# A linear attention and a squared-ReLU MLP on one core: where query loads, key-value products and output stores stand in the program

## The chip, the core and the metric

The kernel runs on one core of a Trainium2 chip. The core has a matrix engine (TensorE, PE in the profile), three engines for elementwise work (VectorE or DVE, ScalarE or ACT, GpSimd or POOL), a SyncE (SP) that in this kernel does nothing but issue transfers, and 16 DMA engines that carry them out. The metric is the device time of one execution in microseconds (us); lower is better. All data are fp32 (the two weight matrices arrive as float64 and are converted in the kernel).

## The reference

Two stages, one after the other, over 8 batches of 576 tokens, 8 heads of 64:

```python
kv  = np.einsum('bhsd,bhse->bhde', k, v)            # per batch and head: 64 x 64
out = np.einsum('bhsd,bhde->bhse', q, kv)
rms = np.sqrt(np.mean(out * out, axis=-1, keepdims=True) + 1e-06)
x   = out / rms * g_norm                            # then (B,H,S,D) -> (B*S, H*D): 4608 x 512
h   = x @ w_in                                      # 512 -> 2048
y   = np.maximum(h, 0.0) ** 2 @ w_out               # 2048 -> 512
```

## The kernel before, in words

**Strips.** The 4608 tokens are 36 tiles of 128, and 4 tiles make a strip; there are nine strips, s = 0 to 8. Each strip runs an up part (x times w_in) and a down part (the squared activations times w_out). Both are Strassen-like products: seven block products in place of eight. Strip 0 uses one level (plain in the up part), strip 1 one level up and two levels down, strips 2 to 8 two levels in both parts. The up part of a strip from 2 on has 55 slots (`up_slot`): slot 7n + 2i holds the i-th small product (8 matmul records in the trace) of set n, so each slot issues one or two of them, and PE needs 0.89 us for one. The down part has 14 steps (`down_deep`), two for each of seven products p in the order 4, 1, 2, 6, 5, 7, 3. Product p = 4 is begun inside the up part (slots 49, 51 and 53), and the last products of p = 3 run in slots 1, 3 and 5 of the next strip.

**Streamed weights.** Sums of weight blocks are computed once, written to DRAM and streamed back for each strip (`stream`, L787): seven transfers of 768 KB for the up part (L793), and for each p one of 768 KB (L799, `w_blk<-w_out`) and one of 1024 KB (L805, `w_blk<-w_deep`). There are four places for them, so a transfer waits on SP until PE has read the tile that was in its place. In the up part `stream()` is called in slots 5, 10, 17, 24 (the rest of the up weights), 31 (w_out of p = 4), 38 (w_deep of p = 4), 45 and 52.

**Attention beside it.** The attention of later tiles is a list of `slices`, written out by hand at L623 to L652, and `attend` (L655) hands them out between the steps: in strips 2 to 8 between slots 1 and 37, up to a goal (L1183) that also limits how many are handed out by each strip. In short:

- `T (b, p)` = `transposed_query`: query of batch b, head pair p, is transposed, for b >= 2 by DVE (L360); with p = 3 of an odd batch also the remaining 64 tokens of two batches (L364, `qT_rest`).
- `K (b, p...)` = `key_value`: k times v for one or two head pairs (L394), eight matmul instructions for 512 tokens and two for the last 64 tokens of the batch (`k_rest`, `v_rest`). After its last product it issues the loads of the next k and v, and with p = 3 `load_rest` for the next batch.
- `query`: q times kv for two tiles (`products_x`, L426), optionally with a K behind it; `mean_roots`, `normalized`: the rms and the scaling on DVE.
- `squares_x`, `send_x` (L570), `fetch_x` (L576): x is transposed through DRAM: DVE transposes 32 x 32 blocks, one transfer writes the tile, four read it back.

The last two slices of a batch's queries and the first of the next one stand so:

```python
        for pair in query_pairs(b):
            ahead = b + 1 < B and pair == query_pairs(b)[-1]
            slices.append((query, (pair, *((b + 1, 0, 1) if ahead else ()))))
...
            if ahead:
                fetch(1)
                slices.append((K, (b + 1, 2, 3)))
```

**Loads.** The pool `qkv` has two places each for q, k and v (L81). For b >= 2 a query tile is four transfers of 64 KB (L121: 32 partitions, rows of 128 bytes). They are not issued where they are asked for, but put on a list (`drip_queries`, L189) by T, two halves per tile, and handed out one half per step by `drip` (L183); the remaining tokens' queries (L167, `q_rest`) go on a second list. In the up part a half of a query load goes out at every slot as long as there is one, in the down part at every second step:

```python
                if i < n_up or i % 2:
                    drip(s == DEEP or i % 2 == 1)
```

`k_rest` holds two batches, one in each half of the partitions. The products over it run over all 128 partitions; `v_rest` has a copy for each parity whose other half is zero (memsets at L320 and L321), so that the other batch's half adds nothing.

**Outputs.** `out_rows` (L661) says which rows of the result the two tiles of an output block go to. For batches from 2 on the tokens of a tile are permuted in blocks of 32, and a block of two tiles is sent as four transfers (one per 32 partitions, 64 KB each), for each of four column and token halves of a strip.

**One queue.** All of these, weights, q, k, v, x and outputs, are issued by SP in program order. An issue that has to wait for a place holds up everything behind it.

## Time and profile before

| what | us |
|---|---|
| five runs | 937.71, 931.76, 932.73, 936.63, 933.51 |
| median | 933.51 |
| the profiled execution, whole | 937.71 |
| its span, first to last instruction | 935.9 |
| outside the span | 1.8 |
| PE busy in the span | 891.3 |
| DVE, ACT, POOL busy | 731.9, 318.5, 305.4 |

The profiled execution is the slowest of the five. The profile names groups of instructions by line, engine, operation and tiles (out<-in); it also lists who waited for whom, a timeline for each engine, and for stretches of time the busy time of each engine with the clock that PE was granted (1.00 is full speed) and the mean share of the 16 DMA engines in use. An entry "SPq" is the issue of a transfer, not the transfer: the time beside it is SP's, and the median time from issue to landing is a table of its own. An SP entry with x8 covers eight issues one after the other. Matmul records overlap by their pipelining, so the distance from one group's start to the next group's start tells more than the duration shown. Over half of the chain of work that ended last is PE in the lines of the up part and the down part (L1109 and L921).

### The profile page before, as it was taken

To read this page: it belongs to the slowest core of one execution; us is meant where nothing else is said; L and a number is where in the kernel's file an instruction comes from. 1 tells how busy PE (TensorE), PEld (TensorE's weight loads), DVE (VectorE), ACT (ScalarE), POOL (GpSimd) and SP (SyncE) were. 2 spreads that over 40 slices of the span, in tenths; PEclk is the share of its full clock that TensorE was granted. 3 is DMA by queue.
4 is the path that set the end of the run, shared out by engine and by line. 5 is a ranking of instruction groups with operands and counts; after the bars stand their busy time and mean duration, and the time that the engine had idled before them with its cause. 6 is when DMAs were issued, how large, how long until landed. Compare 5 with 4: busy or idle time off the path is not lost.

```text
span 935.9 us, 20822 instructions
## 1 busy us (share of the span) xinstructions
PE 891.3 (95%) x8246; PEld 831.8 (89%) x8246; DVE 731.9 (78%) x1258; ACT 318.5 (34%) x638; POOL 305.4 (33%) x315
## 2 busy tenths in 40 slices
PE   6999799899999999989999999869999999999998
PEld 5534688789989999989999999869999999999998
DVE  3899779678867996769678967649689957985886
ACT  3797432221025502360137012710155015302710
POOL 0000000920248404630456045510463147234700
PEclk8999899999999999999999999979999999999999
DMA  8689998979898696878877886868655875685375
GB/s 267 212 290 262 289 334 271 265 246 366 302 229 256 243 317 205 217 228 318 277 188 249 330 269 178 212 235 319 232 181 200 329 228 181 257 300 170 140 291 194
DMA packets 173810, 235.74 MB, mean 252 GB/s; under 512 B 85008, under 2 KB 138768, under 8 KB 165264
## 3 DMA queue, kind: packets, MB, share of 16 engines
q1 hardware_dynamic: 173392, 234.27, 77.2%
q8 instruction: 65, 1.06, 0.5%
q14 instruction: 33, 0.27, 0.1%
q10 hardware_dynamic: 320, 0.13, 0.1%
HBM read 197.66 MB, written 36.70 MB: 250 GB/s over the span
## 4 chain that ended last, share of the span: by engine, by line
PE 70%; DVE 14%; DMA 7%; issue 3%; SPq 3%; ACT 1%; POOL 1%; DVEq 0%; ACTq 0%; POOLq 0%
PE ps_B L921 21%; PE ps_A L921 16%; PE ps_A L1109 15%; PE ps_B L1109 7%; PE ps_C L1109 4%; DMA w_blk<-w_deep 2%; PE ps_A L700 2%; PE x_ps L426 2%; DVE gt L1121 2%; PE kv_ps L394 1%; DVE w_c L250 1%; SPq L121 1%; DVE snap L1121 1%; DMA w_out<-w_in 1%; DVE w_t L270 1%
## 5 line engine op out<-in xcount | busy, mean ns | idle before, releaser
L921 PE MATMUL ps_B<-w_blk,g_s 128*128 128x128 f32 x1024 | 127.5, 277 | 0.0
L921 PEld LDWEIGHTS ps_B<-w_blk,g_s 128*128 128x128 f32 x1024 | 121.8, 194 | 0.0
L921 PE MATMUL ps_B<-w_blk,gt 128*128 128x128 f32 x768 | 99.1, 278 | 11.4 <-DMA w_blk<-w_deep 10.8
L1109 PE MATMUL ps_A<-x_l,w_in 128*128 128x128 f32 x784 | 107.1, 281 | 0.3 <-ACT snap L1126 0.3
L921 PEld LDWEIGHTS ps_B<-w_blk,gt 128*128 128x128 f32 x768 | 92.6, 194 | 12.3 <-issue 11.1
L270 POOL TENSOR_TENSOR x_l<-xT 128x256 f32<-128x256 f32 x21 | 15.4, 736 | 262.1 <-PE ps_A L921 203.4
L1109 PEld LDWEIGHTS ps_A<-x_l,w_in 128*128 128x128 f32 x784 | 97.9, 196 | 1.0 <-ACT snap L1126 0.5
L921 PE MATMUL ps_A<-w_blk,g_s 128*128 128x128 f32 x768 | 93.6, 275 | 0.0
L921 PEld LDWEIGHTS ps_A<-w_blk,g_s 128*128 128x128 f32 x768 | 89.6, 192 | 0.0
L1121 POOL TENSOR_TENSOR snap<-snap,gt 128x512 f32<-128x512 f32 x35 | 45.8, 1310 | 126.6 <-ACT snap L1126 93.5
L1059 ACT ACTIVATE gt<-gt 128x512 f32<-128x512 f32 x112 | 69.6, 622 | 28.2 <-DVE gt L1121 28.2
L1126 ACT COPY snap<-ps_A 128x512 f32<-128x512 f32 x63 | 36.6, 582 | 122.6 <-PE ps_A L1109 109.4
L921 PE MATMUL ps_A<-w_blk,gt 128*128 128x128 f32 x576 | 72.2, 275 | 0.0
L1060 ACT ACTIVATE gt<-gt 128x512 f32<-128x512 f32 x112 | 70.6, 631 | 3.6
L936 DVE TENSOR_TENSOR o_sb<-o_sb,ps_B 128x256 f32<-128x256 f32 (+1 forms) x128 | 49.4, 386 | 26.7 <-ACT o_sb L937 19.4
L921 PEld LDWEIGHTS ps_A<-w_blk,gt 128*128 128x128 f32 x576 | 68.2, 192 | 0.0
L1121 DVE TENSOR_TENSOR gt<-ps_A,gt 128x512 f32<-128x512 f32 x49 | 32.8, 681 | 43.0 <-PE ps_A L1109 41.3
L1019 POOL TENSOR_TENSOR w_i<-w_in 128x512 f32<-128x512 f32 x7 | 9.3, 1332 | 161.6 <-DVE w_in L270 160.6
L1121 POOL TENSOR_TENSOR gt<-gt,snap 128x512 f32<-128x512 f32 x42 | 52.3, 1273 | 23.5 <-DVE snap L1121 23.5
L270 DVE TENSOR_TENSOR gt<-gt 128x2048 f32<-128x2048 f32 (+1 forms) x29 | 59.7, 2063 | 0.0
L937 ACT COPY o_sb<-ps_A 128x128 f32<-128x128 f32 x24 | 6.4, 265 | 145.7 <-PE ps_A L921 145.7
L1109 PE MATMUL ps_A<-x_l,w_blk 128*128 128x128 f32 x392 | 53.3, 280 | 1.8 <-POOL x_l L270 0.9
(176 smaller groups left out, 1842.6 us busy)
## 6 DMA issues: line engine op xcount, KB each, us to landing
w_blk<-w_deep SPq DMA_DIRECT2D x56, 1024.0 KB, 6.0
w_blk<-w_out SPq DMA_DIRECT2D x56, 768.0 KB, 5.6
w_blk<-w_in_deep SPq DMA_DIRECT2D x49, 768.0 KB, 5.2
raw<-in_moe_w_in_dram SPq DMA_DIRECT2D x16, 512.0 KB, 6.5
raw<-in_moe_w_out_dram SPq DMA_DIRECT2D x16, 512.0 KB, 6.3
k<-in_k_dram SPq DMA_DIRECT2D x29, 256.0 KB, 4.6
v<-in_v_dram SPq DMA_DIRECT2D x29, 256.0 KB, 4.9
x_d<-x_q SPq DMA_DIRECT2D x27, 256.0 KB, 3.7
```

The costliest lines, as they stand in the source:

```text
L121: eng.dma_start(out=t[ts(a, SQ)], in_=src[b, 2 * p + h, 0 : C * P, f : f + SQ].rearrange("(i k) f -> i k f", k=4 * C),)
L250: yield nc.vector.scalar_tensor_tensor(out=ci, in0=high, scalar=-(2**30), in1=ci, op0=ALU.bitwise_and, op1=ALU.bitwise_or)
L270: eng.tensor_tensor(out=out, in0=a, in1=b, op=ALU.subtract)
L426: nc.tensor.matmul(ps[half, r, i, ts(p, D)], lhsT=q[row, half], rhs=kvd[b, p][row, row], start=True, stop=True)
L700: nc.tensor.matmul(bank[BANK[p]][:, i, :], lhsT=lhsT(k), rhs=rhs(k), start=p in (1, 5, 2) and i == 0 and k == 0, stop=k == n - 1, skip_gro ...
L921: nc.tensor.matmul(chain[c][x][:, i, :], lhsT=a[:, f, :], rhs=w[:, f, :], start=x not in opened[c] and f == 0, stop=f == FQ // 2 - 1, skip ...
L936: add = lambda out, a, b: nc.vector.tensor_tensor(out=out, in0=a, in1=b, op=ALU.add)
L1059: nc.scalar.activation(o, o, AF.Relu)
L1060: nc.scalar.activation(o, o, AF.Square)
L1109: nc.tensor.matmul(ps[:, i, :], lhsT=w, rhs=rhs, start=j in (1, 2, 5) and i == 0, stop=True, skip_group_check=True)
L1121: add = lambda eng, out, a, b: eng.tensor_tensor(out=out, in0=a, in1=b, op=ALU.add)
L1126: nc.scalar.copy(t, ps)
```

## The change

Six edits, which together move instructions and change few: the number of matmuls is the same.

```diff
-                t = qkv_pool.tile([P, 4 * C, SQ], FP32, name=n, tag=n) if 0 in parts else main[n, b, p]
+                t = qkv_pool.tile([P, 4 * C, SQ], FP32, name=n, tag=n, bufs=3) if 0 in parts else main[n, b, p]
...
-    v_rest = const.tile([P, 2, H, D], FP32, name="v_rest")
+    v_rest = const.tile([P, H, D], FP32, name="v_rest")
...
-    nc.vector.memset(k_rest, 0.0)
-    nc.vector.memset(v_rest, 0.0)
...
+        if (b, p) == (1, NP - 1):
+            drip_queries()
...
-                    a, w = (tk[:, h, c, :], tv[:, h, c, :]) if c < C else (k_rest[:, 2 * p + h], v_rest[:, b % 2, 2 * p + h])
+                    a, w = (t[:, h, c, :] if c < C else r[half, 2 * p + h] for t, r in ((tk, k_rest), (tv, v_rest)))
...
-    slices += [(features, (last[0],)), (T, (2, 2)), (K, (2, 2, 3)), (T, (2, 3))]
+    slices += [(features, (last[0],)), (T, (2, 2)), (T, (2, 3)), (K, (2, 2, 3))]
     for b in range(2, B):
+        pairs = query_pairs(b)
+        for i, pair in enumerate(pairs):
+            left = len(pairs) - i
+            more = b + 1 < B
+            keys = (b + 1, *{2: (0, 1), 1: (2, 3)}[left]) if more and left < 3 else ()
+            fetch(1)
+            if i == 0 and b > 2:
+                slices += [(T, (b, p)) for p in (2, 3)]
+            slices.append((query, (pair, *keys)))
+            if more and left == 1:
+                slices.append((T, (b + 1, 1)))
             slices.append((mean_roots, (pair,)))
             fetch(1)
             slices.append((normalized, (pair,)))
+            if more and left == 2:
+                slices.append((T, (b + 1, 0)))
...
-                to += [(ts(k, SQ), both, rows[k, :, cs]) for k in range(4)]
+                to += [(slice(0, P), slice(t + j, t + j + 1), rows[:, :, c]) for j, c in enumerate(range(cs.start, cs.stop))]
...
-            goal = max(goal, min(ready[DEEP_UP] + 24 * (s - 1), *ahead[:1], len(slices)))
+            goal = max(goal, min(ready[DEEP_UP] + 22 * (s - 1), *ahead[:1], len(slices)))
...
-                if i < n_up or i % 2:
-                    drip(s == DEEP or i % 2 == 1)
+                if i % (2 if s == DEEP else 4) == 1 and i < min(n_up, 37) or i >= n_up and i % 3:
+                    drip(True)
```

In words: q has three places; the products over the last 64 tokens read only their own half of the partitions, with one `v_rest` and no memsets; K of the next batch goes with the last two queries of the batch in front, pairs 0 and 1 with the last but one and pairs 2 and 3 with the last, in place of pairs 0 and 1 with the last and pairs 2 and 3 behind it; a half of a query load goes out at every fourth slot up to slot 37 (every second step in strip 1) and at two of three steps of the down part; the goal of slices grows by 22 per strip in place of 24; and a block of two output tiles goes out as two transfers of 128 KB, one per tile, over all partitions, whose target is a pattern of 4 x 32 rows of 256 columns.

## The prediction

> **What bounds the kernel now.** The page first: PE is busy nearly the whole span, so time can only come out of the 44.6 us (935.9 - 891.3) in which it waits, and out of stretches in which it runs slowly.

> ```profile
> PE 891.3 (95%) x8246; PEld 831.8 (89%) x8246; DVE 731.9 (78%) x1258; ACT 318.5 (34%) x638; POOL 305.4 (33%) x315
> ```

> Then the list of waits of PE alone: whom it waited for, total, times, longest. Four of its larger entries are transfers or DVE work that the change moves.

> ```profile
> PE ps_B L921 <- DMA w_blk<-w_deep: 10.8, 2, 7.6
> PE kv_ps L394 <- DMA v_rest<-in_v_dram: 3.5, 2, 2.7
> PE kv_ps L394 <- DMA v<-in_v_dram: 3.3, 3, 1.3
> PE x_ps L426 <- DVE qT_rest L364: 1.9, 1, 1.9
> ```

> Third, the timeline of PE around the longest one, in strip 5. Look at the distance of starts: eight matmuls of this kind need 0.89 us elsewhere.

> ```profile
> 584.18 0.69 PE L394 MATMUL kv_ps<-v,k 128*64 128x64 f32 x16
> 587.53 0.34 PE L394 MATMUL kv_ps<-v_rest,k_rest 128*64 128x64 f32 x4 [2.66 <-DMA v_rest<-in_v_dram]
> ...
> 588.38 1.92 PE L1109 MATMUL ps_A<-x_l,w_blk 128*128 128x128 f32 x8
> 590.09 1.91 PE L1109 MATMUL ps_A<-x_l,w_in 128*128 128x128 f32 x8
> ...
> 607.98 1.06 PE L1109 MATMUL ps_B<-x_t,w_blk 128*128 128x128 f32 x8
> 616.64 2.05 PE L921 MATMUL ps_B<-w_blk,gt 128*128 128x128 f32 x8 [7.61 <-DMA w_blk<-w_deep]
> 618.48 1.92 PE L1109 MATMUL ps_A<-x_l,w_in 128*128 128x128 f32 x8
> 620.18 4.95 PE L921 MATMUL ps_B<-w_blk,g_s 128*128 128x128 f32 x32
> ```

> A wait costs more than itself. After the 2.66 us wait the next groups of eight start 1.71, 1.71 and 0.99 us apart: 1.7 us lost (0.82 + 0.82 + 0.10). After the 7.61 us wait it is 1.84, 1.70 and 4.79 (to 624.97) for 8, 8 and 32: 3.0 us lost; the windows give PE a clock of 0.81 in 600 to 620 us and 1.00 before the waits. After the third long one, 3.21 us at 410.8 in strip 3, it is 1.39, 1.71 and 3.96: 1.7 us lost. After the 1.86 us wait at 267 nothing is lost. [...]

> Fourth, why w_deep came late: SP's timeline.

> ```profile
> 581.62 0.63 SPq L153 DMA_DIRECT2D v_rest<-in_v_dram  x1
> ...
> 583.01 9.14 SPq L121 DMA_DIRECT2D q<-in_q_dram  x8
> ...
> 601.66 7.85 SPq L121 DMA_DIRECT2D q<-in_q_dram  x8
> 609.55 2.04 SPq L576 DMA_DIRECT2D xT<-x_d  x4
> 611.69 0.38 SPq L805 DMA_DIRECT2D w_blk<-w_deep  x1
> ```

> This w_deep is asked for in slot 38, whose matmuls start at 595.47; it is issued 15 us after the end of that slot, behind two bunches of eight query loads (9.1 and 7.9 us of SP). Strip 3 has the same picture: eight q between 395.25 and 402.72, xT x8 at 402.76, w_deep at 408.87. The bound that can be moved is thus SP's queue; PE's work cannot be.

> **The change, part by part.** The sum is for the profiled execution (937.7).

> *Strip 5, w_deep of p = 4: -10.6* (7.6 + 3.0). In the changed order only two query issues, two x_d and four xT stand between w_out (slot 31) and w_deep (slot 38): 2 x 0.62 + 2 x 0.38 + 4 x 0.45 = 3.8 us, plus up to 3.7 us (median landing of x_d) that xT waits. Slot 38 is 6.2 us (seven slots of 0.89) after slot 31 and 13.4 before slot 53, which needs the tile; with its median landing of 6.0 us it may be issued 7 us late. No more than four query loads stand in a row anywhere after strip 1.

> *Strip 3, the same: -4.9* (3.2 + 1.7). More stands there: xT x4, K's four loads, two rest loads, q x2, xT x4 = 1.8 + 1.7 + 1.3 + 1.2 + 1.8 = 7.8 us, again from slot 31: at most some 2 to 5 us late of 7. If that cover goes, the old stall returns here first.

> *Strip 5, K of batch 7: -4.4* (2.7 + 1.7). Its loads were issued from 578.3 on, nine us after their places came free, behind xT and q. In the changed kernel K (6, 2, 3) is in slot 9 and K (7, 0, 1) in slot 25, 14 us apart, with x_d and xT right ahead of the six loads; issue 3.0 and landing 5.8 fit.

> *Strip 2, qT_rest: -1.9.* T (3, 3) moves from slot 6 to slot 3, so on DVE it stands ahead of the output sums of slot 5, which hold it at 267.96 now; DVE idles from 258.5 to 263.1. The query itself moves to slot 5, PE at 264. Strip 1's first w_out: -0.5, by less in front of it.

> *Strip 1, K of batch 3: a new wait, +2.3.* Now K (2, 2, 3) waits twice, 1.29 and 0.93 us at 173.7 and 175.8, since its loads stand behind eight query issues; behind four, and one step later (1.73 us), it does not: -2.2. But K (3, 0, 1) now follows K (2, 2, 3) after one step and 64 small products (1.73 + 1.16 us), and takes its places. The rows of now for these very loads:

> ```profile
> 176.22 0.59 SPq L130 DMA_DIRECT2D k<-in_k_dram  x1
> ...
> 179.23 0.63 SPq L153 DMA_DIRECT2D v_rest<-in_v_dram  x1
> ```

> Three us from first to last issue. With K (2, 2, 3) from 175.4 to 176.7, PE is at K (3, 0, 1) by 179.6; v_rest, issued about 178.8, lands at 184.6 (median 5.8). PE waits 1.8 us for v, then again for v_rest: 4.5 us in all (2.5 if they land as fast as the k and v of batch 2 did, 6.2 with a slow clock behind it). I take 4.5. Queued behind on PE is the up part of strip 1; ACT and DVE wait with the query's squares, for which five PSUM places leave room.

> *The other edits.* The products over 64 rows are as many as before; I take 0 between -1 and +1, as x_ps runs on 64 rows at 64 products per 1.16 us. The memsets end at 2.5 us, before their loads are issued (3.3): 0. Query loads in the streamed part: three halves and four q_rest pairs in strips 3 and 5, 3 x 1.25 + 4 x 0.9 us of SP between issues that are 2.7 to 3.6 us apart, fits; but DMA is 0.84 to 0.94 busy there. A weight tile is issued 8.7 to 9.8 us before its use (239.18 and 242.75 for the product at 248.97 and its second half at 251.5) and lands in 5.6 to 6.0: about 3 us of slack. I take +2 in all (0 to +7). The small waits of PE on DVE, ACT and POOL, 4.1 us together, move with everything; 0, between -2 and +2.

> *Outputs.* Two issues in place of four, 0.42 us each on SP (its median): with four blocks in a strip, 8 x 0.42 = 3.4 us less for SP per strip, hidden but for the terms above. Their transfers: 128 KB from 128 partitions landed in 4.6 us (median), 64 KB from 32 in 4.2. At the end of the kernel -0.5 to +2; I take +0.5. [...]

> Sum: -10.6 - 4.9 - 4.4 - 1.9 - 0.5 + 2.3 + 2 + 0.5 = -17.5, thus 920.2 for an execution like the profiled one. That one is the slowest of five, 4.2 us over the median; I assume that half of this lies in the stalls that go, as they hang on landing times, and take 2.1 off: **918**.

> **The rivals.**

> *Given back in the streamed parts.* If output transfers or query loads hold DMA engines that weights need, the 3 us of slack goes. [...] With 1.3 us lost in each of eight streamed parts and 2 at the end: 937.7 - 20 + 12.4 = 930. For it: DMA at 0.94 in strip 1. Against: SP waits for PE ahead of most weight issues, so the queue is not behind.

> *Slower.* The same place, but with each wait above 2 us, so that PE drops its clock each time: 2.2 + 1.7 us in eight parts and 2 at the end, 937.7 - 20 + 33 = 951. It decides from about 1.2 us past the slack of 3.

> *The bunches only change place.* x_d and xT wait for DVE and for landings, and SP stands still with w_deep behind them as now; the 20 us of stalls stay and strip 1 gets its new one: about 936. For it: xT waited 23 us for x_d in this trace. Against: x_d is asked for seven slots after the query, where it was four.

> **How the numbers follow.** Forecast 0.72 (909: all terms at their best and the whole 4.2 off; 931: all at their worst and nothing off), given back 0.13, only moved 0.08, slower 0.07. Range: 909 to 931, which leaves out the last two. A measurement of this kernel can tell 0.5% (4.7 us) from no change. Faster by more: 0.72 and 0.06 of the second case, 0.78; slower 0.08; between 0.14.

> **What would show it.** w_deep gone from PE's waits in strips 3 and 5, no group of eight 1.7 us apart there; v_rest gone at batch 7 and come at batch 3 (strip 1) with 3 to 5 us; no qT_rest. Wrong if PE waits in the streamed parts, or if SP issues w_deep of p = 4 more than 7 us after slot 38.

## The result, and the profile after

The changed kernel takes 930.66 us (median of 53 runs, 925.09 to 936.12), the kernel before 934.68 us (median of 95 runs, 924.16 to 945.66). The ratio is 0.9967, 95% interval 0.9955 to 0.9980. That is some 3 to 4 us faster, where 15.5 had been forecast.

The profiled execution took 930.17 us (span 928.4). The page's busy line, for the changed kernel:

```profile
PE 887.9 (96%) x8246; PEld 826.3 (89%) x8246; DVE 729.7 (79%) x1256; ACT 319.2 (34%) x638; POOL 305.6 (33%) x315
```

PE still has 40.5 us in which it waits (928.4 - 887.9), against 44.6. The list of waits of PE (in total, times, longest) says which ones went and which came. L923 and L395 here are L921 and L394 of before:

```profile
PE ps_B L923 <- DMA w_blk<-w_deep: 6.5, 4, 2.9
...
PE kv_ps L395 <- DMA v_rest<-in_v_dram: 3.8, 2, 2.6
...
PE ps_A L923 <- DMA w_blk<-w_deep: 1.3, 2, 1.1
...
PE ps_B L923 <- DMA w_blk<-w_out: 1.0, 2, 0.7
...
PE x_ps L427 <- DVE qT_rest L362: 0.2, 1, 0.2
```

The two waits for w_deep of 3.2 and 7.6 us are gone, and qT_rest is down from 1.9 us to 0.2. In their place are many short ones. Most are in the streamed part of strip 1, as the timeline of PE shows:

```profile
219.69 2.02 PE L923 MATMUL ps_B<-w_blk,gt 128*128 128x128 f32 x16 [0.65 <-DMA w_blk<-w_out]
...
223.13 1.16 PE L923 MATMUL ps_B<-w_blk,gt 128*128 128x128 f32 x8 [0.53 <-DMA w_blk<-w_deep]
...
227.65 2.02 PE L923 MATMUL ps_A<-w_blk,gt 128*128 128x128 f32 x16 [0.69 <-DMA w_blk<-w_out]
...
231.72 1.16 PE L923 MATMUL ps_A<-w_blk,gt 128*128 128x128 f32 x8 [1.15 <-DMA w_blk<-w_deep]
```

The timeline of SP for the same stretch shows what stood between the weights:

```profile
213.97 0.91 SPq L807 DMA_DIRECT2D w_blk<-w_deep  x1
214.92 4.63 SPq L121 DMA_DIRECT2D q<-in_q_dram  x4
219.65 2.73 SPq L571 DMA_DIRECT2D x_d<-x_q  x1
222.42 0.43 SPq L801 DMA_DIRECT2D w_blk<-w_out  x1
...
225.31 4.74 SPq L577 DMA_DIRECT2D xT<-x_d  x4
231.74 0.34 SPq L801 DMA_DIRECT2D w_blk<-w_out  x1
```

Between the issues at 213.97 and 222.42 no weight goes out. The issue of x_d takes 2.7 us there (the next one, at 223.44, takes 0.38), so SP is held up at the issue itself; by what, the profile does not show.

The table cuts the time at matmuls that all kernels have. "Last group" is the first matmul of p = 3, the last of a strip; the stretch "p = 4" runs from its first matmul to that of p = 1 and takes 8.93 us without waits. The second execution of each kernel is from the experiments below. The stretches that are left out differ by 1.2 us together.

| us | before | before, again | changed | changed, again |
|---|---|---|---|---|
| start to strip 1 | 156.14 | 152.56 | 153.28 | 151.86 |
| strip 1: up part | 60.98 | 64.85 | 66.41 | 68.24 |
| strip 1: streamed part to the last group | 37.94 | 37.90 | 43.30 | 43.89 |
| **last group of strip 1, at** | **255.06** | **255.31** | **262.99** | **264.00** |
| to p = 4 of strip 2 | 55.88 | 55.88 | 54.25 | 54.25 |
| p = 4 of strip 2 | 9.76 | 9.79 | 12.06 | 13.68 |
| p = 4 of strip 3 | 14.00 | 10.72 | 9.03 | 9.53 |
| strip 4's last group to p = 4 of strip 5 | 59.39 | 60.74 | 53.66 | 53.66 |
| p = 4 of strip 5 | 19.67 | 17.38 | 10.54 | 10.23 |
| strip 5's last group to the last matmul | 275.49 | 275.50 | 277.12 | 277.34 |
| last matmul to the end | 4.17 | 4.19 | 7.47 | 7.48 |
| span | 935.89 | 931.56 | 928.38 | 934.02 |

Between the first profiled executions, strips 3 and 5 gain 19.8 us (14.00 - 9.03, 59.39 - 53.66, 19.67 - 10.54) and qT_rest 1.6. Against that, strip 1 ends 7.9 us later, p = 4 of strip 2 takes 2.3 us more, the rest after strip 5 takes 1.6 more, and the end 3.3.

### The profile page after: what moved, and what is told of

Read it like the earlier page. It is cut to its first block, busy times and chain, and to the rows that moved or that the text cites. A ratio compares the mean times of both kernels' runs of the same rounds, so it can differ in the third digit from the quotient of the medians.

```text
span 928.4 us, 20668 instructions
## 1 busy us (share of the span) xinstructions
PE 887.9 (96%) x8246; PEld 826.3 (89%) x8246; DVE 729.7 (79%) x1256; ACT 319.2 (34%) x638; POOL 305.6 (33%) x315
## 3 DMA queue, kind: packets, MB, share of 16 engines
q8 instruction: 65, 1.06, 0.5%
## 4 chain that ended last, share of the span: by engine, by line
PE 76%; DVE 10%; DMA 8%; issue 2%; ACT 1%; SPq 1%; DVEq 0%; ACTq 0%
PE ps_B L923 19%; PE ps_A L1111 17%; PE ps_A L923 15%; PE ps_B L1111 9%; PE ps_C L1111 4%; PE ps_A L702 4%; DMA w_blk<-w_deep 3%; PE kv_ps L395 2%; PE x_ps L427 2%; DVE w_c L250 2%; PE ps_B L702 2%; PE ps_C L702 1%; DMA w_out<-w_in 1%; DVE ms L444 1%; DMA q<-in_q_dram 1%
## 5 line engine op out<-in xcount | busy, mean ns | idle before, releaser
L923 PE MATMUL ps_B<-w_blk,g_s 128*128 128x128 f32 x1024 | 126.0, 275 | 0.0
L923 PEld LDWEIGHTS ps_B<-w_blk,g_s 128*128 128x128 f32 x1024 | 120.0, 192 | 0.1
L923 PE MATMUL ps_B<-w_blk,gt 128*128 128x128 f32 x768 | 98.0, 276 | 7.5 <-DMA w_blk<-w_deep 6.5
L1111 PE MATMUL ps_A<-x_l,w_in 128*128 128x128 f32 x784 | 104.1, 276 | 0.3
L270 POOL TENSOR_TENSOR x_l<-xT 128x256 f32<-128x256 f32 x21 | 15.4, 734 | 258.0 <-PE ps_A L923 191.4
L923 PEld LDWEIGHTS ps_B<-w_blk,gt 128*128 128x128 f32 x768 | 91.4, 192 | 8.8 <-issue 4.6
L1111 PEld LDWEIGHTS ps_A<-x_l,w_in 128*128 128x128 f32 x784 | 95.4, 192 | 1.0 <-DVE snap L1123 0.5
L923 PE MATMUL ps_A<-w_blk,g_s 128*128 128x128 f32 x768 | 93.6, 275 | 0.0
L923 PEld LDWEIGHTS ps_A<-w_blk,g_s 128*128 128x128 f32 x768 | 89.6, 192 | 0.0
L923 PE MATMUL ps_A<-w_blk,gt 128*128 128x128 f32 x576 | 72.4, 275 | 2.0 <-DMA w_blk<-w_deep 1.3
L923 PEld LDWEIGHTS ps_A<-w_blk,gt 128*128 128x128 f32 x576 | 68.2, 192 | 2.6 <-DMA w_blk<-w_deep 1.7
```

The source lines that it names most:

```text
L270: eng.tensor_tensor(out=out, in0=a, in1=b, op=ALU.subtract)
L923: nc.tensor.matmul(chain[c][x][:, i, :], lhsT=a[:, f, :], rhs=w[:, f, :], start=x not in opened[c] and f == 0, stop=f == FQ // 2 - 1, skip ...
L1111: nc.tensor.matmul(ps[:, i, :], lhsT=w, rhs=rhs, start=j in (1, 2, 5) and i == 0, stop=True, skip_group_check=True)
```

## The experiments

Times are medians, with the ratio to the kernel before and its interval from runs on the same chip. The first theory: strip 1 loses 5.8 us because keys times values of batch 3 wait, and 5.3 us because query loads stand in front of the weights; strip 2 loses because six loads of keys and values stand in front of w_deep; the end loses through the new outputs.

The single repairs are too small for the medians: their intervals overlap that of the changed kernel (0.9955 to 0.9980). They are read from the stretches of one profiled execution each. Their spread can be told for strip 1, whose program is the same in the changed kernel and in three of the runs (the old outputs and the two for strip 2): its last group comes at 261.4 to 264.0 us in these five executions, and at 254.2 to 255.3 in three of the kernel before.

### The outputs: taken back, and alone

Outputs as before in the changed kernel (the other way round in the kernel before):

```diff
-                to += [(slice(0, P), slice(t + j, t + j + 1), rows[:, :, c]) for j, c in enumerate(range(cs.start, cs.stop))]
+                to += [(ts(k, SQ), both, rows[k, :, cs]) for k in range(4)]
```

> The changed kernel with its outputs as before: four transfers of 32 partitions for each block in place of two whose outermost size is 4. Theory: from the last matmul to the end the changed kernel needs 7.5 us where the kernel before needed 4.2, because the last transfers land 1.4 us apart; that goes, 3.3 us, and no more than 1 us beside it, since SP gets 3.4 us of issues a strip back: 926.5 us, 0.991 of the kernel before. First rival: the transfers hold engines that weights need, so the waits in strips 5 to 8 (1.3 us each) go as well: 922. Second rival: the end only waits for the order of the last products, nothing goes: 930.5.

Measured: 927.95 us, 0.9939 (0.9909 to 0.9968). The last matmul ends where it did (921.3 against 920.9), and from there to the end it takes 4.11 us instead of 7.47. The theory holds. The first rival does not: from strip 5's last group to the last matmul it takes 277.05 us with the old outputs and 277.12 with the new ones, so the weights there lose nothing to them.

> The kernel before with the new outputs alone. Theory: the end 3.3 us later, the rest as before: 938, ratio 1.0035. First rival, engines held from weights: 1.3 us more in each of eight streamed parts, 948, ratio 1.014. Second rival: SP, freed of 3.4 us of issues a strip, gets to w_deep of p = 4 earlier in strips 3 and 5 and gives the 3 us back: 934.5, ratio 1.000.

Measured: 941.84 us, 1.0068 (1.0035 to 1.0100), thus about 6 us slower. The end takes 7.11 us, 2.9 more. The rest lies in the same stalls, which are longer in this execution:

```profile
PE ps_B L921 <- DMA w_blk<-w_deep: 12.8, 3, 8.2
```

This was 10.8 in the first execution of the kernel before and 8.0 in its second. How much of it the outputs cause and how much is the spread of single executions stays open; the medians' interval, 3.3 to 9.4 us, begins just above the 2.9 of the end. From strip 5's last group to the last matmul nothing is lost here either (275.48 us against 275.49). The gain for SP that the second rival supposed is not there.

What the transfers do is seen at the very end, in the view of the DMA in 40 slices of 0.375 us (busy share of 16 engines in tenths, GB/s). The kernel before, 921 to 936 us:

```profile
DMA  7999977211110000000445643455420007990000
GB/s 197 393 415 371 371 328 284 87 44 44 44 44 22 0 0 0 0 0 0 106 109 137 169 134 115 123 156 161 120 68 0 0 0 191 249 249 11 0 22 0
```

The changed kernel, 914 to 929 us:

```profile
DMA  0000000000122222222222222222222221000000
GB/s 0 0 0 0 0 0 0 0 0 0 27 35 90 93 98 90 96 93 82 96 96 87 85 96 98 96 93 98 98 96 96 98 93 68 0 0 0 0 0 22
```

In the changed kernel the share stands at 0.2 and the rate at 82 to 98 GB/s for nearly eight us without a break; the windows give 0.27 and 94 GB/s from 918.5 to 926.4 us. That is about a quarter of the 16 engines' time, while outputs queue for it. Of the last six outputs the first four land 1.4 to 1.5 us apart, 128 KB each; before, 64 KB landed every 0.48 us. The trace's semaphore record has 10496 updates for 689 transfers, which is 5 for each of the 48 with this pattern and 16 for each of the others (48 x 5 + 641 x 16); in the trace of before, all 761 transfers have 16. Of the 5 updates of each of the last six, one comes 0.95 to 1.41 us after the start of the issue and the other four from 3.3 us after it on.

### Keys times values of batch 3, late in strip 1

```diff
+            if b == 2:
+                keys = (3, 0, 1) if left == 1 else ()
...
+            if b == 2 and left == 1:
+                slices.append((K, (3, 2, 3)))
```

> The changed kernel with keys times values of batch 3 back at the places of before (the first two pairs with the last query of batch 2, the last two at the end of strip 1), query loads spread as changed. Theory: the waits of 1.1 and 2.6 us at keys times values of batch 3 and the slow matmuls after them go, 5.8 us of the up part of strip 1, while the 5.3 us of its streamed part stay, as the query loads in front of the weights stay: 925, 0.989 of the kernel before. First rival: the streamed part loses its time through the same bunch, so 9 to 11 us go: 920.5. Second rival: the wait comes back at the end of strip 1, where K stands in front of the weights: 931.

Measured: 930.31 us, 0.9944 (0.9919 to 0.9968). The up part of strip 1 takes 60.2 us instead of 66.4, as expected. But the streamed part takes 49.2 instead of 43.3, and the last group comes at 263.2, as in the changed kernel (263.0). One wait alone has 5.1 us:

```profile
PE ps_B L927 <- DMA w_blk<-w_out: 5.1, 1, 5.1
```

The theory falls, and the second rival fits: PE reaches the weights 6 us earlier and waits for them 6 us longer, the 5.1 us at the third w_out, in front of which SP now has the six loads that keys times values issue. What sets the end of strip 1 is not PE's waits ahead of it. The table above says the same of the kernel before: its strip 1 begins at 156.14 and 152.56 (and at 149.82 in the run with the new outputs), and its last group comes at 255.06, 255.31 and 254.22. Six us at the start make one at the end.

### The query loads of strip 1, earlier and fewer

One drip in every step, as before the change; then also none after step 18, which leaves the two loads of batch 4 to strip 2:

```diff
-                if i % (2 if s == DEEP else 4) == 1 and i < min(n_up, 37) or i >= n_up and i % 3:
+                if i % 4 == 1 and i < min(n_up, 37) or i >= n_up and i % 3 or s == DEEP and i < n_up:
```

> The changed kernel with one drip of query loads in every step of strip 1's up part, as before the change, so that the rest of queries 3 is loaded there too and nothing of the queries stands between the weights of its streamed part except the two loads that the third place lets in (batch 4, pair 0). Late keys took nothing off strip 1: its last product group came at 263.0 us with and without the early keys, as the weights set that time. Theory: the weights stand behind eight query issues and eight rest issues that are asked for too late; with those earlier the streamed part of strip 1 begins with its weights loaded, and the group that came at 263.0 comes at 257 to 259 us (255.1 in the kernel before); keys times values of batch 2 wait 2 us again; 926. Rival: the transfers as such fill the DMA engines in strip 1 (query loads have packets of 128 bytes, and two more queries are loaded there), whatever their order: the group stays at 262 to 263, 930.

Measured: 931.16 us, 0.9976 (0.9940 to 1.0011), last group at 264.6.

```diff
-                if i % (2 if s == DEEP else 4) == 1 and i < min(n_up, 37) or i >= n_up and i % 3:
+                if (i < 19 if s == DEEP else i % 4 == 1 and i < min(n_up, 37) or i >= n_up and i % 3):
```

> As the run before this one, and without the two loads that the third place lets in: no drip after step 18 of strip 1, so that the loads of batch 4, pair 0, come in strip 2. Theory: these are the loads that still stand in front of the weights; the last group of strip 1 is within 1.5 us of the kernel before, 255 to 257 us, and the whole 924, if strip 2 takes the two loads without loss. Rival, DMA as a whole: 259 to 261.

Measured: 928.27 us, 0.9940 (0.9911 to 0.9969), last group at 262.6; its profiled execution took longer (span 930.3) than the median. This theory falls too; the first rival, transfers as such, fits: the order of the query loads alone moves the last group by less than 2 us. In both, the streamed part takes 38 to 39 us, nearly as before the change, and the up part 71 to 74: keys times values of batch 2 and of batch 3 now both wait for their loads behind the queries (7.5 us in the second run), and in the first one the strip's first w_out is waited for 4.5 us, which the table's cut counts with the up part. The sum is the same.

### The loads that keys times values bring along

What all these kernels have in common are the loads. Each call of key_value issues the next k and v. With all of batch 3 in strip 1, four loads of 256 KB and two rest loads of 128 KB, which were asked for in strip 2, are asked for in strip 1. Over the strip, transfers in the changed kernel run at 273 GB/s (the view from 145 to 265 us); 1.31 MB at that rate are 4.8 us. Two kernels take them out: one moves keys times values back entirely, the other moves the loads alone:

```diff
+                if b == 3 and p >= 2:
+                    continue
                 load_next(names="kv")
...
+                if s == 2 and i == 0:
+                    for _ in range(2):
+                        load_next(names="kv")
+                    load_rest(4, nc.sync)
```

> The changed kernel with only the loads moved: keys times values of batch 3 stay early in strip 1, but the four loads and two rest loads that its last two pairs issue are asked for in slot 0 of strip 2. Theory, the loads as such: the waits at keys times values of batch 3 stay (3.6 us), the streamed part loses no more than 2 us instead of 5.3; last group at 258 to 260, 927. Rival, the order of the query loads: 262 to 263, 930.5.

Measured: 929.49 us, 0.9947 (0.9916 to 0.9978). The last group comes at 257.9, 5.1 us earlier, in the size of the 4.8 us. Keys times values wait as they did; the weights of the streamed part no longer do, but for 1.1 us:

```profile
PE ps_B L925 <- DMA w_blk<-w_deep: 5.9, 3, 3.1
...
PE kv_ps L395 <- DMA v_rest<-in_v_dram: 3.2, 2, 2.2
```

The theory holds for the place: the six loads cost strip 1 these 5 us. In the median this kernel cannot be told from the changed one. The 3.1 us are the wait in p = 4 of strip 2, which PE now reaches 5 us earlier; with the slow matmuls after it, p = 4 takes 13.9 us there instead of 12.1, which gives back a part.

What the loads cost with is not settled, since this edit takes bytes and issues out together. SP's timeline in the changed kernel, and then in this one:

```profile
199.07 2.05 SPq L577 DMA_DIRECT2D xT<-x_d  x4
202.20 0.40 SPq L130 DMA_DIRECT2D k<-in_k_dram  x1
...
205.87 0.63 SPq L153 DMA_DIRECT2D v_rest<-in_v_dram  x1
206.60 0.57 SPq L1024 DMA_DIRECT2D w_in_deep<-w_i  x1
...
213.50 0.43 SPq L801 DMA_DIRECT2D w_blk<-w_out  x1
```

```profile
199.04 2.04 SPq L579 DMA_DIRECT2D xT<-x_d  x4
201.18 0.38 SPq L1026 DMA_DIRECT2D w_in_deep<-w_i  x1
...
208.28 0.44 SPq L803 DMA_DIRECT2D w_blk<-w_out  x1
```

In the stretch before 201 us the two agree to 0.5 us. Then the six loads hold SP for 5.4 us (1.1 of it before the first one goes out), and the weights behind them are issued 5.1 to 5.4 us later, up to the third w_out. So the time on SP fits the 5.1 us as well as the 4.8 us of transfers do. For the transfers speaks that the 16 engines are in use nearly all the time there: their mean share is 1.00 from 205 to 225 us and 0.94 from 225 to 245, and without the loads still 0.95 and 0.93. No run moves the issues without the bytes.

The other one adds to the edit with late keys:

```diff
             if b == 2 and left == 1:
+                fetch(1)
                 slices.append((K, (3, 2, 3)))
...
+        goal += s == 2
```

> The changed kernel with keys times values of batch 3 entirely as before: the first two pairs with the last query of batch 2, the last two in strip 2, so that the four loads and two rest loads that these issue (1.25 MB) are out of strip 1 as well; strip 2 takes one slice more and so ends where it did. So far strip 1's last group came at 260 to 265 us in each kernel that has all keys times values of batch 3 in strip 1, wherever they stood there and however the query loads were spread, against 254 to 255 in the two that have not. Theory: it is the loads that come with them, which share the DMA engines with the strip's weights; the group comes at 256 to 259 (the two query loads of the third place and their late order are left), and 925. Rival: the query loads in front of the weights: 262 or more, 930.

Measured: 930.11 us, 0.9960 (0.9929 to 0.9992), last group at 256.8. Strip 1 answers as expected, but the 6 us are lost again: strip 2's up part takes 3.1 us more (57.32 against 54.25), and w_deep waits 4.1 us in strip 5, where this kernel's slices run one behind.

### Strip 2: what stands in front of w_deep

First all of strip 2 ends one slice earlier (`goal -= s == 2`), so that the query and keys times values go to strip 3; then only that slice moves, to slot 40, and strip 3 stays as it was:

> The changed kernel with the slices of strip 2 ending one earlier, so that the query of block 17 and the last keys times values of batch 4 stand at the head of strip 3, behind w_deep of p = 4 on SP. Theory: w_deep is issued some 3.5 us earlier, its wait of 2.9 us in strip 2 and the slow clock after it (1.7) go, and 0 to 2 us come back at the head of strip 3: 927, ratio 0.992. Rival: w_deep comes late for its own transfer of 8.3 us and the wait stays at 2 us or more: 930.5.

Measured: 930.22 us, 0.9949 (0.9919 to 0.9978). The wait in strip 2 goes (9.83 us for p = 4), and strip 3, one slice behind, gets one of 2.7 us (13.53). The bunch only changed its place.

```diff
-                    attend(begun + (goal - begun) * min(i + 1, 38) // 38)
+                    n = begun + (goal - begun) * min(i + 1, 38) // 38
+                    attend(min(n, goal - 1) if s == 2 and i < 40 else n)
```

> The changed kernel with one slice moved: the query of block 17 with the last keys times values of batch 4 from slot 37 of strip 2 to slot 40, behind w_deep of p = 4 on SP, and everything of strip 3 as it was. Theory: the six loads that the keys times values issue no longer stand in front of w_deep; the wait of 2.9 us in strip 2 goes or falls under 0.7, and nothing comes back in strip 3 (it did where the whole strip was moved by one slice): 927. Rival: w_deep is late for xT's wait on x_d: it stays at 2 to 3 us, 930.

Measured: 927.57 us, 0.9929 (0.9902 to 0.9956). SP's timeline in the changed kernel, and then in this one:

```profile
309.27 2.68 SPq L577 DMA_DIRECT2D xT<-x_d  x4
311.99 0.43 SPq L130 DMA_DIRECT2D k<-in_k_dram  x1
...
314.71 0.64 SPq L153 DMA_DIRECT2D v_rest<-in_v_dram  x1
315.45 0.57 SPq L807 DMA_DIRECT2D w_blk<-w_deep  x1
```

```profile
309.37 1.89 SPq L577 DMA_DIRECT2D xT<-x_d  x4
311.30 0.43 SPq L807 DMA_DIRECT2D w_blk<-w_deep  x1
311.82 0.40 SPq L130 DMA_DIRECT2D k<-in_k_dram  x1
```

w_deep is issued 4.2 us earlier, p = 4 takes 8.93 us in strips 2 and 3, and nothing comes back. The theory holds; xT's wait for x_d, the rival, costs nothing once the six loads are behind.

### The repairs together

> The last two runs and the old outputs together. Theory: the sum of what they give alone, 3 us at the end, 6 to 7 in strip 1, 3 to 4.5 in strip 2: 917 to 919, ratio 0.982. Rival: what is won in strips 1 and 2 is lost again in strips 3 and 5, whose weights then stand behind the same loads: 923 or more.

The last two runs meant here are the one with no drip after step 18 of strip 1 and the one with the slice in slot 40. Measured: 921.90 us, 0.9869 (0.9837 to 0.9901); strip 1's last group at 260.2. That lies between theory and rival; the six loads are still in strip 1.

In the next kernel the loads of keys and values are in strip 2, w_deep of strip 2 stands first, the outputs are as before, and the drips of strip 1 are these:

```diff
+                if ((i > 7 or i % 2) and i < 20 if s == DEEP else i % 4 == 1 and i < min(n_up, 37) or i >= n_up and i % 3):
```

> The same four repairs, but with keys times values of batch 3 left where the change put them and only their loads asked for in strip 2. Theory: 2 to 5 us over the kernel with late keys, for the waits at keys times values of batch 3: 918 to 920. Rival: the same as that kernel, if the waits are only moved: 916.

Measured: **919.32 us, 0.9840 (0.9810 to 0.9870)**. The last group of strip 1 comes at 256.5, the end takes 4.11 us. Of the waits, those of keys times values of batch 3 are the largest left in the strips:

```profile
PE kv_ps L395 <- DMA v_rest<-in_v_dram: 3.9, 2, 2.9
...
PE kv_ps L395 <- DMA v<-in_v_dram: 2.0, 1, 2.0
PE ps_A L925 <- DMA w_blk<-w_out: 1.5, 1, 1.5
```

The kernel that this one was expected to follow has the late keys of i_keys3_as_before instead, and drips up to step 20:

> Keys times values of batch 3 as before, the drips of strip 1 doubled from step 8 on and stopped after step 20 (so the rest of queries 3 is loaded before the weights and batch 4, pair 0, in strip 2), the last keys times values of batch 4 behind w_deep in strip 2, and the old outputs. Theory: strip 1's last group at 254 to 256 as in the kernel before, no wait in strips 2, 3 and 5 above 1 us, 3 us less at the end: 914 to 917, ratio 0.979. Rival: what leaves strip 1 comes back in strip 2: 920 or more.

Measured: 924.25 us, 0.9886 (0.9849 to 0.9924). Strip 1's last group comes earliest of all, at 252.8, yet the whole is slower than with early keys: in strip 5 PE waits 1.3 us for w_out and 4.5 for w_deep. Strips 4 and 5 of this kernel run one slice behind. The next one has the slices of strips 3 to 8 where l_j_best has them:

```diff
-            goal = max(goal, min(ready[DEEP_UP] + 22 * (s - 1), *ahead[:1], len(slices)))
+            goal = max(goal, min(ready[DEEP_UP] + 22 * (s - 1) + 1, *ahead[:1], len(slices)))
```

> The kernel with late keys, with the slices of strips 3 to 8 at the slots of the kernel with early keys. Theory: the 5.8 us in strip 5 came from the one slice by which everything ran behind there (the query's squares on DVE, then x_d, xT and w_deep); with it gone, w_deep of strip 5 waits under 1 us, and the 3 to 5 us at keys times values are saved beside it: 914 to 917. Rival: early keys cost nothing in the end, since the time comes back in the weights of strips 1 to 5: 919.

Measured: **916.38 us, 0.9812 (0.9774 to 0.9850)**, the fastest. p = 4 of strip 5 takes 10.4 us instead of 16.2, so that one slice did cost the stall. Whether late keys beat early ones is not settled: the intervals overlap, and in the profiled executions the kernel with late keys is the slower (918.8 against 917.0). Without the waits at keys times values PE stands 4.8 us at strip 1's first w_out instead, and the last group comes at 256.3.

### The two kernels once more

> The kernel before, unchanged. If the 3.2 us of the first 145 us are a matter of single executions, the first product after that mark comes between 143 and 147 us here too (148.75 in the first profiled execution of this kernel, 145.58 in that of the changed one); if the change won them, at 148 or 149. The long waits of strips 3 and 5 stay within 1.5 us of 3.2 and 7.6.

Measured: 933.35 us. Strip 1 begins at 152.56, so the head start of the changed kernel was one of single executions. Two of the stalls that the change removes are shorter here:

```profile
PE ps_B L921 <- DMA w_blk<-w_deep: 8.0, 2, 6.4
...
PE kv_ps L394 <- DMA v_rest<-in_v_dram: 2.8, 2, 1.9
```

> The changed kernel, unchanged. Theory: the last group of strip 1 at 260 to 265 us, a wait of 1.5 to 3 us for w_deep in strip 2, 7 to 8 us from the last matmul to the end. If these were accidents of one execution, they are not there.

Measured: 935.80 us, near the top of its range. Last group of strip 1 at 264.0, 2.9 us for w_deep in strip 2, 7.5 us at the end: none of the three is an accident.

## Why the prediction was wrong

**Where it was right.** Strips 3 and 5 were forecast at -10.6, -4.9 and -4.4, together -19.9; the first profiled executions give -19.8. That it comes out to 0.1 is in part luck: the second executions of the two kernels give -15.4. For qT_rest -1.9 were forecast and -1.6 found. Keys times values of batch 3 were forecast to wait 4.5 us and wait 3.6 (3.9 in the second execution), v and then v_rest, as worked out.

**The step that failed: strip 1.** The prediction had "+2 in all (0 to +7)" for the streamed parts, +2.3 for keys times values and -0.5 for the first w_out. It put at nothing that the call of keys times values for the last two pairs of batch 3 brings four loads and two rest loads, 1.31 MB, into strip 1. For strip 3 it had priced such a set (1.7 + 1.3 us of SP); here it counted neither issues nor bytes, nor saw that strip 1's end hangs on its queue of transfers already before the change. The slack of "about 3 us" was read at 239 us, after that stretch; the tiles ahead of it showed the opposite, with landings of 8 to 12 us (w_deep issued at 211.89 landed at 220.07, the one at 213.56 at 225.13). Nor is SP "not behind" there, which spoke against the first rival. In place of +3.8 stand 7.9 us at the last group. Late keys and early query loads changed nothing of it; moving the loads took 5.1 off. Whether they cost through their bytes or through SP's time stays open. The rival "given back in the streamed parts" named the kind of place and the time (930), but not the mechanism, and the time is luck: it put the loss on outputs and queries in eight parts, and the largest part lies in strip 1 and on loads of keys and values. Strip 1's outputs do not have the new pattern yet.

**The outputs.** Taken at +0.5, with +2 as the worst; found +3.3 in the profile, 2.9 when added alone and 3.4 when taken back. No row of before has that pattern, so landings of 4.6 us for 128 KB and 4.2 for 64 KB could not tell what it costs. Nor does any run show the 2 us at the end that two of the rivals add, or the 1.3 and 2.2 us that they add in each of eight streamed parts: in their place the runs showed about 3 us at the end, and nothing from strip 5's last group to the last matmul (277.05 us with the old outputs, 277.12 with the new ones).

**Strip 2.** Strips 3 and 5 were followed slot by slot, strip 2 only for qT_rest. But the third rival, "the bunches only change place", came true in this one strip: xT, four loads of keys and values and two rest loads in front of w_deep, +2.3 us (+3.9 in the second execution). Its criterion of 7 us after slot 38 was not applied there. It would have given a warning and little more: slot 38's matmuls end at 308.30, w_deep is issued 7.2 us later, and with a landing of 6.0 us PE would have waited 0.5. The transfer took 8.3, which made the wait 2.9.

**The base.** The profiled execution of before lay 3 us above the median, and 2.1 were taken off. The second execution bears that out: p = 4 in strips 3 and 5 is 3.3 and 2.3 us shorter, so part of the -19.9 was only there in the first one.

Added up for the first profiled executions: -17.5 forecast for the span's part and -7.5 found, 10.0 missing. Strip 1 makes 4.1 of it (7.9 less 3.8, and that with the head start of 2.9 us at its beginning), the outputs 2.8, strip 2 2.3, the stretch after strip 5 1.6 (a wait of 1.1 us for ACT's copy that all kernels with the changed slices have), and the small rest takes 0.8 back. With strip 1, strip 2 and the outputs repaired the kernel takes 919 or 916 us, where 918 had been forecast: the gain is there, and the change itself gave most of it back.

## What to carry to other kernels

Moving a call moves all that it issues: count the bytes of its loads in the stretch where they go, and their issues, and ask of that stretch whether its end follows the compute engine or the queue of transfers. A sign of the latter is that its end stays put in executions whose beginnings differ by several us, as in strip 1 before the change, with either outputs (begun at 149.8 to 156.1 us, last group at 254.2 to 255.3). Where a stall is moved by reordering, follow every strip through the new order, not only those that had the stall; and where a transfer gets a pattern that no row shows, let a run decide: the last outputs here, whose pattern begins with 4, kept 0.27 of the engines busy, at 94 GB/s.

## What the runs showed of the hardware

The price of a wait of PE jumps. In p = 4 of the deep strips, single waits for w_deep of 1.17 to 1.73 us cost 0.24 us beside themselves (nine cases). Waits of 1.89, 2.73, 2.74, 2.88, 3.11, 3.21 and 4.09 us cost 1.86 or 1.87. But one of 2.89 us, in the changed kernel's first execution, cost 0.24, while one of 2.88 at the same place in the second cost 1.87. The longest ones, of 4.4 to 8.2 us, cost 2.0 to 3.1. The clock that PE was granted (the third number from the end) differs just behind these two, first the wait of 2.89, then that of 2.88:

```profile
324.00:326.00 2.00, 2.00 (x19) 2.00 (x20) 0.08 (x1) 0.00 (x0) 0.00 (x0) 1.00 0.82 285
```

```profile
325.00:327.00 2.00, 2.00 (x11) 2.00 (x12) 0.00 (x0) 0.00 (x0) 0.00 (x0) 0.51 0.94 379
```
